# A fused attention, expert-attention and gated-MLP kernel: another written order of its pieces, and engines chosen batch by batch

## The chip, the cores and the metric

The kernel runs on one core of a Trainium2 chip. The metric is the device time of one execution in microseconds (us), as the median of several runs. The core has five instruction queues that run beside each other: TensorE (PE, with its weight loads as PEld), VectorE (DVE), ScalarE (ACT), GpSimd (POOL) and SyncE (SP), which issues DMAs. Each takes its own instructions in the order in which the program lists them, and waits on semaphores for what the others have to deliver.

## The reference, cut to what matters

Three layers follow each other, for 8 batches of 576 positions with 512 features. Everything is float32.

```python
# 1. attention, 8 heads of 64: a position sees its own block of 64 and all earlier blocks
scores = np.where(block_i >= block_j, (q @ k.T) / 8, -1e9)
x = softmax(scores) @ v
# 2. four experts, each a causal attention head of 64; the two best by gate, weighted
logits = x @ w_gate
for e in range(4):
    ye = softmax(causal((x @ wq[e]) @ (x @ wk[e]).T / 8)) @ (x @ wv[e]) @ wo[e]
    out += weight_of_e_if_in_top_2 * ye
# 3. gated MLP with a product over positions
h = np.maximum(out @ w_in, 0)
u, v = h[..., :512], h[..., 512:]
v_n = (v - mean(v)) / sqrt(var(v) + 1e-6)
v_s = einsum('ts,bsd->btd', w_spatial, v_n) + b_spatial[None, :, None]
return (u * v_s) @ w_out
```

## The kernel before, in words

Most float32 products are made of float16 halves: a number is cast to a high half, the rest is a low half, and a product is three matmuls (`PROD`). So almost each result passes through a scale or cast, usually on ScalarE, and a subtract on VectorE or GpSimd.

Work is cut into 1416 named steps, and a step into pieces of one engine each (its generator's yields). For each batch `b`, there are six pairs of heads: pairs 0 to 3 are layer 1's eight heads, pairs 4 and 5 layer 2's four experts. In the text a step is named with its batch.

- `load_qk`, `load_v` (lines 250 to 267) load a pair; `mags` (L281, or ScalarE) finds its largest magnitude; `scale1`, `scale2` make powers of two of these.
- `prep_qk` transposes q and k on TensorE (L320) and splits them (L227 on ScalarE, L233 on VectorE). `prep_v` splits v (L229, L231, L233).
- `scores` makes a pair's scores in four parts: matmuls (L369 to L388), maximum on VectorE (L391, L393), its scaling (L401 on ScalarE or L403 on VectorE), exponential on ScalarE (L407, L412).
- `weights` splits the exponentials: a cast (L327 on ScalarE, L329 on VectorE, L331 on GpSimd), and a subtract (L431, on VectorE or GpSimd). `weights_t` transposes them by DMA (L438).
- `av` multiplies by v (L448) and divides by the row sums (L464 to L471). `halves` casts (L480 on ScalarE or L482 on VectorE), subtracts (L484), and transposes by DMA (L486).
- Layer 2's own: `proj` (matmuls L803, then L813 on ScalarE and L816 on VectorE), `vproj` (L826 to L835), `gate` (L842 to L863).
- Layer 3: `hv` (matmuls L882, ScalarE L886, statistics L890 and L892), `norm0` (14 small VectorE instructions, L897 to L911), `norm` in five parts (L920 on VectorE or GpSimd, L923 on ScalarE, L926 on VectorE or GpSimd), `gating` (L961, L965), `gating2` (matmuls L977, then L980, L983, L985), `outp` (L997, L1000 and the store).
- At the start the weights are read, combined and split by steps named `su`: `su.win` and `su.wout` end in two multiplications, L530 and L531, on VectorE or GpSimd.

Nothing is decided while the kernel runs. `ORDER` is a written list of 3766 numbers; each occurrence of a number emits the next piece of that step, and an engine gets its pieces in this order. Steps of neighbouring batches are mixed in it. `WAYS` tells on which engines a step with a choice runs: one letter for one piece (`A` ScalarE, `D` VectorE, `G` GpSimd, `S` SyncE), two letters for cast and subtract. Tiles come from small pools in the order of the list; `duo`, the accumulators in PSUM, has four.

```python
    for i in ORDER:
        t = named[i]
        ...
        run(t)
```

Of the kernel before, what the change touches and what calls it, by code (L numbers as in the profile page):

```python
# [32 lines left out]
def attn_moe_gmlp_kernel(  # L33
# [17 lines left out]
    V, A, G, T = nc.vector, nc.scalar, nc.gpsimd, nc.tensor  # L51
    B, H, S, D = q.shape
# [711 lines left out]
    def dense(b, keep):  # L764
# [517 lines left out]
    def add(name, due, fn, pieces=(), deps=(), after=(), acq=(), rel=(), pdeps=None, way=None):  # L1282
# [7 lines left out]
        t = steps[name] = Step()  # L1290
# [12 lines left out]
        if way is not None:  # L1303
            ws = WAYS.get(t.place, (way,))
            t.way = ws[min(len(ws) - 1, 3 if t.b == B - 1 else min(t.b, 2))]
# [164 lines left out]
    su = startup()  # L1470
# [55 lines left out]
    for i in ORDER:  # L1526
        t = named[i]
# [45 lines left out]
```

## Time and profile before

| what | before |
|---|---|
| median of 3 runs | 1098.11 us (1095.63 to 1103.18) |
| profiled execution | 1096.49 us |
| its span, first to last instruction | 1094.8 us |
| mean granted TensorE clock | 0.933 of full speed |
| TensorE busy | 892.7 us |
| VectorE busy | 832.1 us |
| ScalarE busy | 660.9 us |
| GpSimd busy | 383.4 us |

Busy time is the union of an engine's instructions over the span. A mean over the span hides stages that differ, so stretches are read by themselves. A row of the timeline gives start and duration of some instructions of one kind, and in square brackets how long the engine had been idle before, and what ended that.

### The profile page before, as it was taken

Reading aid. Unit: us, or ns where it says so; the run is one execution under the profiler, and the core shown is the slowest. Engines: PE = TensorE matmul, PEld = TensorE weight load, DVE = VectorE, ACT = ScalarE, POOL = GpSimd, SP = SyncE. Lnnn points to the kernel's source line nnn. Section 1 sums busy time; section 2 is a strip of 40 time slices with the busy share of each in tenths; the row PEclk is TensorE's granted clock in tenths of the full one; section 3 lists DMA queues with packets and bytes.
Section 4 is the critical chain, followed back from the end, with each engine's and each line's share of the span. In section 5 each row is a group of like instructions: output and inputs, shape, how many; then the busy total and the mean of one; then the engine's idle time right before and its main releaser. Section 6 shows DMA issues by size and latency. Waiting matters only on the chain.

```text
span 1094.8 us, 25341 instructions
## 1 busy us (share of the span) xinstructions
PE 892.7 (82%) x10170; PEld 646.5 (59%) x10170; DVE 832.1 (76%) x1730; ACT 660.9 (60%) x1140; POOL 383.4 (35%) x309
## 2 busy tenths in 40 slices
PE   0466667758989799699988888997989989898978
PEld 0245555546566466466666556754767577566644
DVE  2689989999877877867777889768797887757541
ACT  2758566675667555666567668665566764536332
POOL 6054413143154221433252425543354342304210
PEclk9968787888889899899999999998999999999989
DMA  9536989699289786669929997789578537933601
GB/s 223 139 70 145 191 163 181 127 163 172 51 145 157 153 174 119 114 119 173 170 36 171 190 168 120 136 153 184 108 131 157 112 51 101 197 53 61 125 5 44
DMA packets 497719, 143.68 MB, mean 131 GB/s; under 512 B 485440, under 2 KB 491728, under 8 KB 497600
## 3 DMA queue, kind: packets, MB, share of 16 engines
q1 hardware_dynamic: 483760, 134.03, 67.3%
q0 software_dynamic: 2176, 5.25, 1.9%
q10 hardware_dynamic: 11664, 2.76, 1.6%
q8 instruction: 80, 1.31, 0.5%
q14 instruction: 39, 0.32, 0.1%
HBM read 38.19 MB, written 9.44 MB: 44 GB/s over the span
## 4 chain that ended last, share of the span: by engine, by line
PE 26%; DVE 14%; DMA 6%; ACT 6%; issue 4%; SPq 3%; POOL 2%; DVEq 0%; ACTq 0%; POOLq 0%
PE duo L977 5%; PE duo L997 5%; PE duo L448 4%; DMA pT<-p 4%; PE duo L803 2%; PE duo L882 2%; PE duo L826 2%; ACT pf L412 2%; DVE st L391 2%; PE duo L369 2%; PE duo L961 2%; SPq L438 2%; DVE vn L926 1%; DVE bs L890 1%; DVE qk L233 1%
## 5 line engine op out<-in xcount | busy, mean ns | idle before, releaser
L431 POOL TENSOR_TENSOR p<-pf,p 128x1024 f16<-128x1024 f32 (+1 forms) x106 | 205.7, 1943 | 330.5 <-ACT p L327 189.1
L412 ACT ACTIVATE pf<-duo,st,es 128x512 f32<-128x512 f32 (+3 forms) x256 | 139.8, 621 | 75.0 <-DVE st L403 58.9
L448 PEld LDWEIGHTS <-pT 128*128 128x128 f16 x4320 | 149.0, 100 | 30.4 <-DMA pT<-p 13.6
L391 DVE TENSOR_REDUCE st<-duo 128x2 f32<-128x1024 f32 (+1 forms) x192 | 150.5, 813 | 12.0 <-PE duo L377 5.9
L369 PE MATMUL duo<-qk 64*128 64x256 f16 (+3 forms) x1152 | 114.8, 313 | 45.3 <-ACT pf L412 13.6
L977 PE MATMUL duo<-wsp,vn 128*128 128x288 f16 x896 | 121.1, 289 | 10.4 <-ACT vn L923 6.3
L448 PE MATMUL duo<-v,pT 128*128 128x65 f16 (+1 forms) x2880 | 106.8, 198 | 14.6 <-DMA pT<-p 8.6
L997 PE MATMUL duo<-wo,gT 128*128 128x512 f16 (+1 forms) x480 | 111.2, 388 | 6.8 <-DVE xh L484 3.9
L977 PEld LDWEIGHTS <-vn 128*128 128x128 f16 x896 | 86.9, 98 | 35.0 <-ACT vn L923 6.9
L803 PE MATMUL duo<-x,wqk 128*128 128x288 f16 x768 | 102.5, 295 | 4.7 <-ACT pf L412 1.7
L369 PEld LDWEIGHTS <-qk 64*128 64x128 f16 x1152 | 49.4, 97 | 79.5 <-issue 56.8
L803 PEld LDWEIGHTS <-wqk 128*128 128x128 f16 x768 | 76.4, 100 | 27.1 <-issue 5.6
L997 PEld LDWEIGHTS <-gT 128*128 128x128 f16 (+1 forms) x480 | 47.5, 102 | 62.1 <-issue 12.8
L412 ACT ACTIVATE pf<-duo,st,mt 128x384 f32<-128x384 f32 (+3 forms) x128 | 69.8, 618 | 21.4 <-DVE st L403 19.9
L281 DVE TENSOR_REDUCE mst<-nat 128x1 f32<-128x640 f32 (+1 forms) x51 | 53.8, 1060 | 32.7 <-DMA nat<-in_v_dram 28.2
L327 ACT CAST p<-pf 128x1024 f16<-128x1024 f32 (+1 forms) x70 | 65.5, 943 | 12.8 <-DMA pT<-p 11.0
L331 POOL TENSOR_SCALAR p<-pf 128x1024 f16<-128x1024 f32 (+1 forms) x34 | 32.8, 965 | 112.7 <-DMA pT<-p 49.2
L826 PE MATMUL duo<-wvg,x 128*128 128x260 f16 x480 | 61.6, 290 | 8.2 <-DVE st L403 5.8
L320 PE MATMUL duo<-ident,nat 128*128 128x128 f32 (+1 forms) x320 | 53.6, 300 | 17.3 <-DVE xh L484 5.5
L233 DVE SCALAR_TENSOR_TENSOR qk<-duo,scb,qk 128x640 f16<-128x640 f32 (+1 forms) x64 | 52.6, 843 | 13.5 <-ACT qk L227 13.4
L227 ACT ACTIVATE qk<-duo,scb 128x640 f16<-128x640 f32 (+1 forms) x64 | 47.9, 768 | 24.6 <-PE duo L320 20.6
L920 POOL TENSOR_SCALAR vf<-vf,nw 128x512 f32<-128x512 f32 (+1 forms) x29 | 23.8, 831 | 110.7 <-DVE nw L911 90.0
(257 smaller groups left out, 1747.7 us busy)
## 6 DMA issues: line engine op xcount, KB each, us to landing
out_dram<-o SPq DMA_DIRECT2D x16, 512.0 KB, 3.3
nat<-in_q_dram SPq DMA_DIRECT2D x56, 128.0 KB, 3.1
nat<-in_k_dram SPq DMA_DIRECT2D x56, 128.0 KB, 3.1
nat<-in_v_dram SPq DMA_DIRECT2D x50, 128.0 KB, 2.9
wf<-in_moe_w_in_dram SPq DMA_DIRECT2D x8, 512.0 KB, 5.0
pT<-p SPq DMA_TRANSPOSE x144, 5.0
wf<-in_moe_w_out_dram SPq DMA_DIRECT2D x4, 512.0 KB, 4.9
pT<-in_moe_w_spatial_dram POOLq DMA_DIRECT2D x1, 1152.0 KB, 7.9
```

Source lines behind the costliest of these rows:

```text
L233: V.scalar_tensor_tensor(lo, src, scl, hi, op0=OP.mult, op1=OP.subtract)
L281: V.tensor_reduce(s.st[:, a, pr:pr + 1], t[:, a].rearrange("p i c d -> p i (c d)"), op=OP.max, axis=AX.X, apply_absolute_value=True)
L327: A.copy(hi, src)
L369: T.matmul(ph[:, hh, o:o + w], p.q[hs, a, ts], p.k[hs, bb, 0:w], start=i == 0, stop=False)
L391: V.reduce_max(st[:, 0, 2 * c:2 * c + 2], ph[:, :, off[c]:off[c] + P * (c + 1)], axis=AX.X)
L412: A.activation(pf[:, n * hh + off[c]:n * hh + off[c] + w], ph[:, hh, off[c]:off[c] + w], AF.Exp, bias=st[:, 1, 2 * c + hh:2 * c + hh + 1], ...
L431: (V if way[1] == "D" else G).tensor_sub(lo, src, hi)
L448: T.matmul(ps[:, hh, o:o + n], pT[:, col(t, kk):col(t, kk) + P], p.v[:, hh, kk, a:a + n], start=kk == 0 and i == 0, stop=kk == nk - 1 and ...
L803: T.matmul(ps[:, MID + a:MID + a + w], wqk16[:, l, c, 2 * n + i, :], x16[c][:, r, a:a + w], start=m == 0, stop=m == 11)
L826: T.matmul(ps[:, i, :260], x16[d][:, l, P * c:P * c + P], wvg16[:, r, d, :], start=m == 0, stop=m == 11)
L977: T.matmul(ps[:, MID + a:MID + a + n], vn[:, l, ds_], wsp16[:, r, c, a:a + n], start=i == 0, stop=False)
L997: T.matmul(ps[0:r, i], gT[:, x, d, P * c:P * c + r], wo16[:, y, d, :], start=m == 0, stop=m == 11)
```

## The change

The list of numbers is replaced by another with the same numbers, each as often as before. All pieces of a step keep their order. Of 3766 places the first 1375 move little; the sections that differ most are places 1375 to 2000, 2750 to 2875 and 3125 to 3625. `WAYS` gets up to eight entries a step, one for each batch; before, batches 0 and 1 had one each, batches 2 to 6 shared the third, and batch 7 had the fourth.

```diff
-        65, 69, 1, 68, 1, 68, 68, 68, 68, 68, 21, 23, 72, 76, 73, 66, 73, 76, 73, 76, 72, 76, 72, 72, 76, 72,
+        65, 69, 1, 68, 1, 68, 68, 68, 68, 68, 21, 23, 72, 76, 73, 66, 73, 76, 73, 76, 77, 76, 77, 77, 76, 72,
...
     WAYS = {
-        "su.win.0": ("D", "G", "G", "G"), "su.hl.0": ("D", "G", "G", "G"), "su.win.1": ("D", "G", "G", "G"),
+        "su.win.0": ("D",), "su.hl.0": ("D",), "su.win.1": ("G",), "su.hl.1": ("G",), "su.win.2": ("D",),
...
-        "w.3.1": ("DG", "AG", "AG", "DD"), "w.3.2": ("AG", "DG", "AG", "AD"), "w.3.3": ("AD", "AD", "AD", "DD"),
+        "w.3.2": ("AG", "GG", "AG", "AG", "AG", "AG", "AG", "DG"), "w.3.3": ("AD",),
...
-        "norm.2": ("GG", "DD", "GG", "DG"), "norm.3": ("GG", "DG", "GG", "DD"),
+        "norm.2": ("GG", "DG", "GG", "GG", "GG", "GG", "GG", "DD"),
+        "norm.3": ("GG", "DG", "GG", "GG", "GG", "DD", "GG", "DD"),
...
-            t.way = ws[min(len(ws) - 1, 3 if t.b == B - 1 else min(t.b, 2))]
+            t.way = ws[min(len(ws) - 1, t.b)]
```

TensorE keeps all its matmuls. By instruction, the choices of engines come to this:

| line | what | before | after |
|---|---|---|---|
| L431 | subtract of `weights`, GpSimd / VectorE | 106 / 86 | 96 / 96 |
| L327, L329, L331 | cast of `weights`, ScalarE / VectorE / GpSimd | 112 / 46 / 34 | 116 / 40 / 36 |
| L401, L403 | scaled maximum, ScalarE / VectorE | 56 / 136 | 66 / 126 |
| L480, L482 | cast of `halves`, ScalarE / VectorE | 38 / 10 | 44 / 4 |
| L530, L531 | weights' conversion, GpSimd / VectorE | 8 / 16 | 12 / 12 |
| L920 | `norm`, GpSimd / VectorE | 29 / 11 | 27 / 13 |
| L926 | `norm`, GpSimd / VectorE | 28 / 12 | 27 / 13 |
| L985 | `gating2`, GpSimd / VectorE | 20 / 12 | 19 / 13 |

All lines named here stand ahead of the list and have the same number in both files.

Three places follow, as they stand in the instruction queues before and after. The first is VectorE's queue at batch 1's `hv` and `norm0`, beside `scores` of batches 2 and 3. Before:

```order
L464 TENSOR_SCALAR rr<-duo 128x10
L466 RECIPROCAL rr<-rr 128x10
L471 TENSOR_TENSOR duo<-duo,rr 128x2x5x64
L233 SCALAR_TENSOR_TENSOR v<-nat,scb,v 128x10x64
L484 TENSOR_TENSOR xh<-duo,xh 128x2x5x64
L391 TENSOR_REDUCE st<-duo 128x2 x3
L393 TENSOR_REDUCE st<-duo 128x1
L403 TENSOR_SCALAR st<-st,mt 128x2
L403 TENSOR_SCALAR st<-st,mt 128x1
L890 BN_STATS bs_5414<-vf 128x6
L890 BN_STATS bs_5415<-vf 128x6
```

After, from the maximum that comes ahead of the same statistics:

```order
L391 TENSOR_REDUCE st<-duo 128x2
L890 BN_STATS bs_5275<-vf 128x6
L890 BN_STATS bs_5276<-vf 128x6
L892 BN_AGGR mv<-bs_5275 128x2
L892 BN_AGGR mv<-bs_5276 128x2
L403 TENSOR_SCALAR st<-st,mt 128x2
L897 TENSOR_SCALAR nw<-mv 128x5
L281 TENSOR_REDUCE mst<-nat 128x2
L899 TENSOR_SCALAR nw<-nw 128x5
L281 TENSOR_REDUCE mst<-nat 128x1
L901 TENSOR_SCALAR nw<-nw 128x5
L391 TENSOR_REDUCE st<-duo 128x2 x2
```

The statistics (`vf` to `bs`) and the first instructions of `norm0` (`nw`) move ahead of `mags` (`mst`) and of the maxima; the end of `av` (`rr`, `duo`), `prep_v` (`v`) and `halves` (`xh`) of batch 3, which stood ahead, come behind.

The second is VectorE's queue at batch 6's `proj` (L816) and batch 5's `norm` (L926). Before:

```order
L816 SCALAR_TENSOR_TENSOR qk<-duo,mt,qk 128x512
L816 SCALAR_TENSOR_TENSOR qk<-duo,mt,qk 64x64 x2
L926 TENSOR_TENSOR vn<-vf,vn 64x512
L816 SCALAR_TENSOR_TENSOR qk<-duo,mt,qk 128x576
L391 TENSOR_REDUCE st<-duo 128x2
L393 TENSOR_REDUCE st<-duo 128x1
```

After:

```order
L920 TENSOR_SCALAR vf<-vf,nw 128x512
L816 SCALAR_TENSOR_TENSOR qk<-duo,mt,qk 128x512
L816 SCALAR_TENSOR_TENSOR qk<-duo,mt,qk 64x64 x2
L926 TENSOR_TENSOR vn<-vf,vn 128x512
L816 SCALAR_TENSOR_TENSOR qk<-duo,mt,qk 128x576
L926 TENSOR_TENSOR vn<-vf,vn 64x512
L391 TENSOR_REDUCE st<-duo 128x2
```

The L816 of 576 columns moves ahead of the L926 of 64 partitions, and the fourth `norm` (L920 and an L926 of 128 partitions) has come from GpSimd.

The third is ScalarE's queue at batch 7's `scores` of pair 3 (`es`) and batch 6's of pair 5 (`mt`), with `outp` of batch 5 (L1000). Before:

```order
L412 ACTIVATE pf<-duo,st,es 128x384 x2
L412 ACTIVATE pf<-duo,st,es 128x128 x2
L1000 ACTIVATE o<-duo,hs 128x1024
L401 ACTIVATE st<-st,ln_178,es 128x1
L407 ACTIVATE duo<-duo,st,es 128x576
L401 ACTIVATE st<-st,ln_178,es 128x2
L412 ACTIVATE pf<-duo,st,es 128x256 x2
L412 ACTIVATE pf<-duo,st,mt 128x512 x2
```

After:

```order
L412 ACTIVATE pf<-duo,st,es 128x384 x2
L412 ACTIVATE pf<-duo,st,es 128x128 x2
L401 ACTIVATE st<-st,ln_178,es 128x1
L412 ACTIVATE pf<-duo,st,es 128x256 x2
L407 ACTIVATE duo<-duo,st,es 128x576
L480 CAST xh<-duo 128x2x5x64
L327 CAST p_140<-duo 128x640
L1000 ACTIVATE o<-duo,hs 128x1024
```

The exponentials of the last two parts of pair 3 (256 and 576 columns) move ahead of `outp`.

## Rows read from the trace of the kernel before

**Rows 1.** The page, part 1: busy time and share of the span by engine.

```profile
PE 892.7 (82%) x10170; PEld 646.5 (59%) x10170; DVE 832.1 (76%) x1730; ACT 660.9 (60%) x1140; POOL 383.4 (35%) x309
```

**Rows 2.** Windows: stretch, length, then busy us (instructions): PE, PEld, DVE, ACT, POOL; granted clock; DMA.

```profile
48.00:256.00 208.00, 142.63 (x1643) 112.37 (x1643) 191.60 (x350) 136.12 (x239) 74.38 (x53) 0.79 0.79 149
390.00:564.00 174.00, 151.36 (x1825) 109.95 (x1822) 133.56 (x297) 104.75 (x178) 54.73 (x37) 0.97 0.73 132
564.00:753.00 189.00, 165.33 (x2036) 117.73 (x2036) 148.90 (x312) 129.34 (x217) 88.01 (x66) 0.98 0.86 156
753.00:785.00 32.00, 29.99 (x336) 20.89 (x333) 24.74 (x76) 22.32 (x44) 7.81 (x7) 0.94 0.65 127
855.00:1012.00 157.00, 143.71 (x1596) 104.93 (x1591) 115.56 (x247) 90.20 (x165) 47.81 (x38) 0.98 0.58 99
```

**Rows 3.** Groups by line and form: busy us, mean ns, then idle before and releasers.

```profile
L431 POOL TENSOR_TENSOR p<-pf,p 128x1024 f16<-128x1024 f32 x79 | 173.3, 2195 | 255.8 <-ACT p L327 162.3 <-DVE p L329 55.3 <-issue 14.8
...
L431 DVE TENSOR_TENSOR p<-pf,p 128x1024 f16<-128x1024 f32 x17 | 21.9, 1288 | 7.8 <-ACT p L327 5.0 <-POOL p L331 2.0 <-issue 0.8
...
L926 DVE TENSOR_TENSOR vn<-vf,vn 64x512 f16<-64x512 f32 x6 | 14.9, 2486 | 3.3 <-ACT vn L923 3.2
...
L482 DVE CAST xh<-duo 128x640 f16<-128x640 f32 x10 | 8.2, 818 | 0.2
...
L926 DVE TENSOR_TENSOR vn<-vf,vn 128x512 f16<-128x512 f32 x6 | 5.2, 882 | 1.3 <-ACT vn L923 1.3
...
L531 DVE TENSOR_TENSOR x<-x,sg 128x512 f32<-128x512 f32 x6 | 4.2, 692 | 0.6
L530 DVE TENSOR_TENSOR x<-x,e 128x512 f32<-128x512 f32 x6 | 4.1, 685 | 0.1
```

**Rows 4.** Windows around 437 to 450 us, columns as in rows 2.

```profile
410.00:437.00 27.00, 25.00 (x280) 18.16 (x279) 20.97 (x57) 15.23 (x30) 3.70 (x3) 1.00 0.65 121
437.00:450.00 13.00, 3.55 (x23) 1.99 (x24) 12.69 (x32) 8.37 (x14) 4.57 (x2) 0.72 0.15 30
450.00:460.00 10.00, 10.00 (x156) 7.97 (x153) 8.02 (x15) 7.28 (x12) 4.77 (x3) 0.86 1.09 188
```

**Rows 5.** Timeline of PE, 440 to 452 us.

```profile
446.61 0.61 PE L369 MATMUL duo<-qk 64*128 64x512 f16 x2 [4.58 <-DVE qk L233]
449.59 1.04 PE L369 MATMUL duo<-qk 64*128 64x512 f16 x4 [2.36 <-DVE qk L233]
```

**Rows 6.** Timeline of DVE, 436 to 437.5 us.

```profile
436.69 1.27 DVE L890 BATCH_NORM_STATS2 bs<-vf 128x6 f32<-128x512 f32 x2
```

**Rows 7.** Timeline of PE, 890 to 964 us.

```profile
896.66 1.46 PE L369 MATMUL duo<-qk 64*128 64x512 f16 x6 [3.23 <-DVE qk L816]
...
949.98 1.52 PE L448 MATMUL duo<-v,pT 128*128 128x65 f16 x42 [2.74 <-DMA pT<-p]
...
961.43 1.44 PE L448 MATMUL duo<-V,pT 128*128 128x65 f16 x42 [1.69 <-DMA pT<-p]
```

**Rows 8.** Timeline of all engines, 886 to 896 us.

```profile
886.98 3.77 POOL L920 TENSOR_SCALAR vf<-vf,nw 128x512 f32<-128x512 f32 x5 [6.51 <-DVE nw L911]
...
890.72 4.49 POOL L926 TENSOR_TENSOR vn<-vf,vn 128x512 f16<-128x512 f32 x4
891.22 4.54 DVE L926 TENSOR_TENSOR vn<-vf,vn 64x512 f16<-64x512 f32 x1 [0.44 <-ACT vn L923]
...
895.79 0.82 DVE L816 SCALAR_TENSOR_TENSOR qk<-duo,mt,qk 128x576 f16<-128x576 f32 x1
```

**Rows 9.** Timeline of all engines, 1050 to 1060 us.

```profile
1052.15 1.87 DVE L920 TENSOR_SCALAR vf<-vf,nw 64x512 f32<-64x512 f32 x3
1052.22 1.07 POOL L920 TENSOR_SCALAR vf<-vf,nw 128x512 f32<-128x512 f32 x1 [30.23 <-DVE nw L911]
...
1054.00 1.15 PE L977 MATMUL duo<-wsp,vn 128*128 128x288 f16 x3 [5.84 <-ACT vn L923]
...
1057.75 2.34 PE L977 MATMUL duo<-wsp,vn 128*128 128x288 f16 x9 [1.53 <-POOL vn L926]
```

392 rows, old and new, of tables (ORDER, WAYS) are left out of this document.

## The prediction

> **What bounds the kernel now.** I read the page's busy times first. TensorE works 892.7 us, and VectorE 832.1 us, of a 1094.8 us span [rows 1], so no single engine fills it; an average hides two regimes, and the windows by stretch part them [rows 2]. From 48 to 256 us VectorE is busy 191.6 of 208 us (92%) and TensorE only 142.6: VectorE is the limit there. From 390 us on it turns round. TensorE is busy 151.4 of 174 us, then 165.3 of 189, 30.0 of 32, and 143.7 of 157, and VectorE 74 to 79%. From there on the end is set by TensorE's work plus the gaps in it, and an order can win only what lies in those gaps: 22.6 us between 390 and 564, 23.7 between 564 and 753, 2.0 between 753 and 785, 13.3 between 855 and 1012.
>
> The change leaves TensorE's work as it is, to the instruction. What it moves is where pieces stand. I compared the two lists place by place: positions 0 to 1375 (up to 390 us in this trace) move by 1.5 places or less on average, 1375 to 2000 (390 to 564 us) by some 10, 2000 to 2750 (564 to 753 us) by 1 to 2, 2750 to 2875 by 12, 3125 to 3500 (855 to 974 us) by 6. So the stretch 564 to 753, with 12.5% of gaps, is nearly kept, and the terms below are looked for in the others.
>
> **The change part by part.** *Start.* Two pieces of the weights' conversion (`su.win.1`, `su.wout.1`) go from VectorE to GpSimd: two instructions each, 0.685 and 0.692 us [rows 3], 2.75 us in all. Two casts of `halves` (0.818 us each) go to ScalarE: 1.64 us. Against this two weight subtracts of batch 0 come from GpSimd, 1.288 us each: 2.58 us. VectorE is left with 2.75 + 1.64 - 2.58 = 1.8 us less, in the stretch where it is the limit. I take -1.8 us. The ends are 0, if the 16 us in which VectorE does idle there take it, and -1.8. The converted weights lie on GpSimd beside 74.4 us of work in 208, so it has room [rows 2].
>
> *The jam of batch 3.* Between 437 and 450 us TensorE works 3.55 us of 13, while VectorE works 12.69 [rows 4]. The largest waits there are 4.58 and 2.36 us, for L233 of `prep_qk` of pair 3 [rows 5]: it stands in VectorE's queue behind the bn statistics of batch 1 (436.69 us [rows 6]), the 14 small instructions of `norm0`, a score maximum and two normalizations. Just before, from 410 to 437, VectorE was idle for 27.0 - 21.0 = 6.0 us [rows 4]. The new order puts `hv` of batch 1 ahead of `gating`, so that its statistics and `norm0` stand in VectorE's queue before `mags`, and can use that idle time. It pays with five other instructions of VectorE (the end of `av`, `halves` and `prep_v` of batch 3), which move from before the jam into it, about 3 us by the same forms. Nobody on TensorE waits for these soon: their products go to a later pair. The ends are 0 (as much goes in as comes out) and -9.45, TensorE's whole idle time there. I take half of the 6.0 us: -3.
>
> *The transposes of batch 7 and 6.* `av` waits 2.74 us at 949.98 and 1.69 us at 961.43 for transposed weights [rows 7]. The weights come from scores that TensorE computes, and ScalarE exponentiates, after the product `outp` of batch 5. In the new order both pairs' last scores stand ahead of an `outp`: ScalarE's exponential of the third part of pair 3 comes before L1000 of the first `outp`, not behind it. `outp` itself fills TensorE's time later just as well, and its result goes to the output, for which only the buffer waits. I take the whole, -4.4; the ends are 0 and -4.4. What could take it back is GpSimd, which now makes both halves of the first two parts.
>
> *Scores of batch 6.* At 896.66 TensorE waits 3.23 us for L816, the end of `proj` [rows 7]. That instruction stood behind L926, a subtract of 64x512 that took 4.54 us, from 891.22 to 895.76, while GpSimd ran L920 and L926 back to back from 886.98 to 895.21 [rows 8]. The mean of this form is 2.486 us against 0.882 for twice the partitions [rows 3], so VectorE is held up by GpSimd here. Now L816 comes ahead of this L926. But the fourth normalization has gone to VectorE, and its own L926 stands ahead of that same L816: the same kind of hold, by a run on GpSimd that is two instructions shorter. The ends are -3.23, and +1.3 (one more instruction of GpSimd's run, 4.49 us for four, as the later one now meets it). I take -0.5.
> On this the Trainium skill (GPSIMD Engine Reference, 1. Specifications) says that GpSimd's SBUF interfaces are shared with VectorE, with contention for VectorE instructions that have two SBUF inputs. The 4.54 us agrees. By that rule this place would gain nothing, and the sum would be 0.5 us higher; by the plain move it would gain 3.23.
>
> *The rest.* From 753 to 785 TensorE idles 2.0 us: -1, ends 0 and -2.0. Outside the jam, 390 to 564 holds 22.6 - 9.45 = 13.2 us in many short waits: -1, ends 0 and -13.2. In the tail TensorE waits 5.84 and 1.53 us for the last normalization [rows 9]. That goes to VectorE almost whole, but three of its pieces already took 1.87 us there and now there are five, and only the first product comes earlier (1.07 us on GpSimd against about 0.6): -0.4, ends 0 and -1.5. Loads that change queues are asked for tens of us ahead of use: 0.
>
> *New waits.* Re-made stretches make waits of their own. The waits that I named are 1.69 to 4.58 us long; I charge 2 us, ends 0 and 7.8 (4.58 + 3.23).
>
> **The sum**: -1.8 - 3 - 4.4 - 0.5 - 1 - 1 - 0.4 + 2 = -10.1 us. The profiled execution took 1096.49 us, 1.7 more than its span; 1096.5 - 10.1 = 1086.4. The median of the runs is 1.6 us above this execution, so the forecast is **1088**.
>
> **The rivals.** *All named waits go.* The jam gives 9.45, and 1.4 more, since the granted clock was 0.72 in it and 0.86 in the 10 us behind it [rows 4], which at the full level would be 14% of 10 us; the transposes give 4.4, batch 6 gives 3.2, the stretch from 753 gives 2.0, the start 1.8: 22.3 us, so 1074.2, or 1076 on the median's scale. For it: TensorE is the limit behind each of these places, so nothing eats the gain. Against: the jam's work on VectorE is moved, not removed.
> *The gaps come back elsewhere, no change*, 1098. For it: the stretch that is kept has 12.5% of gaps, those re-made 13.0% and 8.5% [rows 2]. They are not worse than their neighbour, so a new order may draw gaps of the same size.
> *Slower: VectorE's new subtracts are held up by GpSimd.* Twelve two-input subtracts move from GpSimd to VectorE, ten of L431 and one each of L926 and L985. If each pays what L926 pays, 2.486 - 0.882 = 1.6 us, that is 19 us; with all of it on the path and no gain 1117, with two thirds 1110. It decides where GpSimd runs without pause beside them, as in `norm` of batch 5. Against it: L431 of 1024 on VectorE took 1.288 us on average over 17 [rows 3], and a hold like that of L926 in more than a few of them would show in this mean; and ten fewer L431 run on GpSimd, at 2.195 us for the large ones [rows 3].
> The Trainium skill's same line, taken as a rule for the whole kernel, is this rival: any subtract that moves may be held, and a run on GpSimd holds all. No other row of this trace shows a hold as long as batch 5's.
>
> **How the numbers follow.** Forecast, 0.46: 1082 to 1094. All named waits go, 0.20: 1068 to 1082. No change, 0.18: 1094 to 1103. Slower, 0.16: 1103 to 1118. A measurement of this kernel tells about 1% from no change, that is 1087 and 1109. Below 1087 lie the 0.20 and 0.19 of the forecast's 0.46: faster 0.39. Above 1109 lies 0.11 of the 0.16. The rest, 0.50, is the same. The ends of all terms together give -35 to +9 us, 1063 to 1107; that all fall one way is unlikely, so the range is 1074 to 1107 and leaves out a third of the second case and most of the last.
>
> **What would show it.** Right: in the jam of batch 3 TensorE's idle time is under 7 us, and `norm0` of batch 1 begins before the scores' maxima; the two waits of L448 for transposes near the end are gone; L816 of batch 6 still waits behind a long L926. VectorE's busy time from 48 to 256 us falls by about 2 us. The tail, from the last `norm` to the end, is within 1 us. Wrong: the waits return under other names in the same stretches, then TensorE's gaps in the four stretches from 390 us on [rows 2], 61.6 us in all now, stay near 60; or VectorE's mean for L431 with two SBUF inputs rises well over 1.3 us, then it is the slower case.

## The result, and the profile after

| | before | after |
|---|---|---|
| median of 12 runs each, same chip | 1098.07 us (1090.91 to 1106.12) | 1088.11 us (1083.28 to 1091.97) |
| ratio, 95% interval | | 0.9907 [0.9886, 0.9928] |
| profiled execution, span | 1096.49, 1094.8 us | 1087.77, 1086.0 us |

The forecast was 1088. The sum agreed with the measurement; most of its terms did not, and that they came out together at the right sum was luck, as the last sections show.

The page after, part 1, and the windows of the same stretches (columns as in rows 2):

```profile
PE 894.5 (82%) x10170; PEld 649.8 (60%) x10170; DVE 832.3 (77%) x1719; ACT 666.3 (61%) x1154; POOL 374.6 (34%) x307
```

```profile
48.00:256.00 208.00, 144.01 (x1631) 113.38 (x1631) 186.70 (x336) 137.51 (x242) 72.94 (x51) 0.78 0.79 148
390.00:564.00 174.00, 154.12 (x1837) 111.56 (x1834) 141.47 (x298) 107.64 (x187) 54.88 (x37) 0.96 0.68 131
564.00:753.00 189.00, 164.80 (x2017) 118.18 (x2015) 151.91 (x309) 125.56 (x212) 81.31 (x64) 0.95 0.84 154
753.00:785.00 32.00, 31.33 (x388) 23.09 (x386) 30.02 (x82) 20.44 (x37) 13.07 (x15) 1.00 0.93 154
855.00:1012.00 157.00, 148.81 (x1685) 110.38 (x1685) 114.52 (x254) 95.53 (x175) 48.11 (x37) 0.99 0.55 99
```

TensorE's busy time is nearly what it was (892.7 us before, 894.5 now). Its gaps in the four stretches from 390 us on were 61.6 us [rows 2] and are 19.9 + 24.2 + 0.7 + 8.2 = 53.0 us: 8.6 less, and the span fell by 8.8. As the prediction said, the gain lies in gaps. The windows have fixed bounds, so the work in them is not quite the same in both traces. Which gaps changed, four views tell.

**The jam of batch 3.** TensorE's timeline and the windows about the jam, whose 13 us lie at 436 to 449 now (before: rows 4, 5):

```profile
437.08 0.90 PE L384 MATMUL duo<-qk 128*128 128x288 f16 x6 [3.66 <-ACT pf L412]
439.39 1.33 PE L320 MATMUL duo<-ident,nat 128*128 128x128 f32 x5 [1.38 <-ACT pf L412]
444.56 1.41 PE L320 MATMUL duo<-ident,nat 128*128 128x128 f32 x5 [3.85 <-DVE xh L484]
446.81 0.61 PE L369 MATMUL duo<-qk 64*128 64x512 f16 x2 [0.83 <-DVE p L431]
448.60 1.04 PE L369 MATMUL duo<-qk 64*128 64x512 f16 x4 [1.18 <-DVE qk L233]
```

```profile
436.00:449.00 13.00, 4.68 (x22) 2.76 (x23) 11.06 (x27) 8.42 (x15) 3.18 (x2) 0.59 0.21 41
```

The two waits of [rows 5] shrank from 6.94 to 2.01 us, but two L320 and an L384 ahead of them wait instead, one of them for L484, which the new order put into the jam. L484's product goes to a later pair, but L484 is also the instruction after which `halves` gives its `duo` back, and L320 writes a `duo`: TensorE waited for the buffer. All waits above 0.5 us here come to 10.9 us; before they came to 11.2 (2.15 and 2.10 beside the two shown). TensorE idles 8.3 of the 13 us; it was 9.45.

In either kernel VectorE is held here: an instruction that runs while GpSimd works takes much longer than its form does elsewhere (a hold, in what follows). VectorE and GpSimd, before and then after:

```profile
442.87 2.80 DVE L920 TENSOR_SCALAR vf<-vf,nw 128x512 f32<-128x512 f32 x2
443.09 4.57 POOL L431 TENSOR_TENSOR p<-pf,p 128x1024 f16<-128x1024 f32 x2 [10.44 <-ACT duo L407]
```

```profile
431.59 2.13 POOL L431 TENSOR_TENSOR p<-pf,p 128x1024 f16<-128x1024 f32 x1 [3.15 <-ACT p L327]
432.04 1.72 DVE L901 TENSOR_SCALAR nw<-nw 128x5 int32<-128x5 int32 x1
...
438.59 2.13 POOL L431 TENSOR_TENSOR p<-pf,p 128x1024 f16<-128x1024 f32 x1 [4.87 <-DVE p L329]
...
439.50 1.24 DVE L904 TENSOR_TENSOR nw<-nw 128x5 f32<-128x5 f32 x1
```

Before, the 14 small instructions of `norm0` took 0.16 or 0.17 us each, and two L920 took 2.80 us together (0.55 each where nothing held them). After, L901 takes 1.72 us and one L904 1.24, and the maxima stand behind L901. Every trace with the new order here has two such holds among these 14 instructions, of 0.90 to 1.72 us. So what `norm0` does earlier, it does beside a busy GpSimd; how much of the jam this makes up was not tested.

**Batch 6's scores.** Timeline of VectorE and GpSimd, against [rows 8]:

```profile
882.59 3.72 POOL L920 TENSOR_SCALAR vf<-vf,nw 128x512 f32<-128x512 f32 x4 [4.56 <-DVE nw L911]
...
884.84 0.84 DVE L926 TENSOR_TENSOR vn<-vf,vn 128x512 f16<-128x512 f32 x1 [0.33 <-ACT vn L923]
886.13 0.82 DVE L816 SCALAR_TENSOR_TENSOR qk<-duo,mt,qk 128x576 f16<-128x576 f32 x1 [0.45 <-ACT qk L813]
886.29 3.38 POOL L926 TENSOR_TENSOR vn<-vf,vn 128x512 f16<-128x512 f32 x3
887.77 2.45 DVE L926 TENSOR_TENSOR vn<-vf,vn 64x512 f16<-64x512 f32 x1 [0.83 <-ACT vn L923]
```

The L926 that I expected to be held ahead of L816 took 0.84 us, beside L920 on GpSimd. L816 came through, the L926 of 64 partitions was held behind it (2.45 us), and the wait of 3.23 us [rows 7] is gone.

**The transposes.** TensorE's waits from 905 to 965 us (before: rows 7):

```profile
916.55 1.88 PE L977 MATMUL duo<-wsp,vn 128*128 128x288 f16 x14 [2.02 <-ACT u L965]
...
938.05 2.75 PE L997 MATMUL duo<-wo,gT 128*64 128x512 f16 x12 [1.25 <-ACT pf L412]
942.90 1.45 PE L448 MATMUL duo<-v,pT 128*128 128x65 f16 x42 [0.53 <-DMA pT<-p]
950.96 0.90 PE L448 MATMUL duo<-V,pT 128*128 128x65 f16 x24 [0.69 <-DMA pT<-p]
953.07 2.02 PE L448 MATMUL duo<-V,pT 128*128 128x65 f16 x42 [1.21 <-DMA pT<-p]
```

The waits of 2.74 and 1.69 us became 0.53, 0.69 and 1.21, and two new ones stand ahead of them: 2.02 us at L977 and 1.25 us at L997. Together 5.7 us, where there were 4.4.

**The tail.** TensorE's waits for the last normalization, against [rows 9]:

```profile
1044.89 0.66 PE L977 MATMUL duo<-wsp,vn 128*128 128x288 f16 x2 [5.31 <-ACT vn L923]
1046.14 0.42 PE L977 MATMUL duo<-wsp,vn 128*128 128x288 f16 x1 [0.59 <-DVE vn L926]
1046.77 0.66 PE L977 MATMUL duo<-wsp,vn 128*128 128x288 f16 x2 [0.21 <-ACT vn L923]
1048.66 2.34 PE L977 MATMUL duo<-wsp,vn 128*128 128x288 f16 x9 [1.23 <-DVE vn L926]
```

7.3 us, against 7.4.

### The profile page after: what moved, and what is told of

It reads as the page before. It is cut to its first block, busy times and chain, and to the rows that moved or that the text cites. A ratio compares the mean times of both kernels' runs of the same rounds, so it can differ in the third digit from the quotient of the medians.

```text
span 1086.0 us, 25340 instructions
## 1 busy us (share of the span) xinstructions
PE 894.5 (82%) x10170; PEld 649.8 (60%) x10170; DVE 832.3 (77%) x1719; ACT 666.3 (61%) x1154; POOL 374.6 (34%) x307
## 4 chain that ended last, share of the span: by engine, by line
PE 33%; DVE 14%; DMA 7%; ACT 6%; issue 4%; SPq 2%; POOL 1%; DVEq 0%; ACTq 0%; POOLq 0%
PE duo L977 7%; PE duo L997 6%; PE duo L448 5%; DMA pT<-p 5%; PE duo L803 4%; PE duo L369 3%; ACT pf L412 2%; PE duo L961 2%; DVE st L391 2%; PE duo L882 2%; PE duo L826 2%; PE duo L320 1%; DMA nat<-in_k_dram 1%; PE duo L384 1%; DMA nat<-in_v_dram 1%
## 5 line engine op out<-in xcount | busy, mean ns | idle before, releaser
L431 POOL TENSOR_TENSOR p<-pf,p 128x1024 f16<-128x1024 f32 (+1 forms) x96 | 187.3, 1954 | 326.3 <-ACT p L327 217.2
L412 ACT ACTIVATE pf<-duo,st,es 128x128 f32<-128x128 f32 (+3 forms) x256 | 139.3, 621 | 65.0 <-DVE st L403 48.1
L448 PEld LDWEIGHTS <-pT 128*128 128x128 f16 x4320 | 151.4, 101 | 29.9 <-issue 12.1
L369 PE MATMUL duo<-qk 64*128 64x256 f16 (+3 forms) x1152 | 117.6, 321 | 29.7 <-ACT pf L412 14.0
L977 PE MATMUL duo<-wsp,vn 128*128 128x288 f16 x896 | 121.7, 290 | 11.2 <-ACT vn L923 5.5
L448 PE MATMUL duo<-v,pT 128*128 128x65 f16 (+1 forms) x2880 | 108.9, 200 | 15.0 <-DMA pT<-p 7.1
L997 PE MATMUL duo<-wo,gT 128*128 128x512 f16 (+1 forms) x480 | 109.2, 383 | 8.5 <-DVE xh L484 3.9
L977 PEld LDWEIGHTS <-vn 128*128 128x128 f16 x896 | 87.1, 99 | 36.2 <-ACT vn L923 6.1
L369 PEld LDWEIGHTS <-qk 64*128 64x128 f16 x1152 | 49.9, 99 | 62.1 <-issue 44.0
L997 PEld LDWEIGHTS <-gT 128*128 128x128 f16 (+1 forms) x480 | 47.2, 101 | 62.5 <-issue 12.3
L412 ACT ACTIVATE pf<-duo,st,mt 128x384 f32<-128x384 f32 (+3 forms) x128 | 69.9, 616 | 15.0 <-DVE st L403 12.1
L331 POOL TENSOR_SCALAR p<-pf 128x1024 f16<-128x1024 f32 (+1 forms) x36 | 36.5, 1014 | 117.3 <-DMA pT<-p 62.6
L327 ACT CAST p<-pf 128x1024 f16<-128x1024 f32 (+1 forms) x71 | 66.5, 947 | 9.1 <-DMA pT<-p 7.1
L320 PE MATMUL duo<-ident,nat 128*128 128x128 f32 (+1 forms) x320 | 56.4, 314 | 17.1 <-DVE xh L484 6.4
L826 PE MATMUL duo<-wvg,x 128*128 128x260 f16 x480 | 57.6, 278 | 11.6 <-DVE st L403 5.8
L384 PE MATMUL duo<-qk 128*128 128x288 f16 x288 | 47.6, 303 | 17.5 <-ACT pf L412 13.2
```

Source lines behind the costliest of these rows:

```text
L320: T.transpose(ps[:, P * c:P * c + r], p.nat[0:r, i, c, :], ident[0:r, 0:r])
L327: A.copy(hi, src)
L369: T.matmul(ph[:, hh, o:o + w], p.q[hs, a, ts], p.k[hs, bb, 0:w], start=i == 0, stop=False)
L384: T.matmul(ps[:, MID + a:MID + a + n], p.q[:, l, 512:640], p.k[:, r, a:a + n], start=i == 0, stop=i == 2 and not (p.moe and a))
L412: A.activation(pf[:, n * hh + off[c]:n * hh + off[c] + w], ph[:, hh, off[c]:off[c] + w], AF.Exp, bias=st[:, 1, 2 * c + hh:2 * c + hh + 1], ...
L431: (V if way[1] == "D" else G).tensor_sub(lo, src, hi)
```

## The experiments

"Old" and "new" are the lists of before and after. Ratios are to the kernel before, run on the same chip; its median was 1099.61 us beside the first four kernels (`e1` to `e4`), 1099.72 beside the next four (`e5` to `e8`), 1101.87 beside the last four (`e9` to `e12`). The ratios are those on record with their 95% intervals; they are not the quotients of two medians, from which they differ by up to 0.2%.

**Order or engines?** `e1_order` has the new list with the old engines, `e2_ways` the old list with the new engines.

```diff
 e1_order:  ORDER = new   WAYS = old
 e2_ways:   ORDER = old   WAYS = new
```

> The new order with the engines of before. If the gain lies in where pieces stand (places), most of it is here: 5 to 9 us under before, ratio 0.992 to 0.995, and the waits of L448 for transposes near 950 and 961 us are short. If it lies in the engines (fewer subtracts on GpSimd that hold VectorE up), this is within 2 us of before.

> The order of before with the new engines. By the places: between 1 us under before and 4 us over it, since ways and order were not made for each other. By the engines: 6 to 10 us under before, and VectorE's mean for L403 and L926 falls.

Measured: 1097.46 us, 0.9974 [0.9948, 1.0000], and 1100.94 us, 1.0004 [0.9981, 1.0027]. Neither half gives the 0.93%. In `e1_order` the fourth normalization of batch 5 is still wholly on GpSimd, whose run then meets VectorE at batch 6's scores after all: VectorE's L897, of 128x5, took 2.09 us at 877.49. So most of the gain needs order and engines together; up to 0.5% may be the order's alone.

**Early or late?** The two lists hold the same pieces up to place 2739 and behind it, so each part can be exchanged.

```diff
 e4_late:    ORDER = old[:2739] + new[2739:]
 e5_early:   ORDER = new[:2739] + old[2739:]
 e6_batch5:  ORDER = old[:2739] + new[2739:2907] + old[2907:]
```

> Order and engines of before up to place 2739 (some 749 us), and the new ones from there to the end. By the places: 7 to 9 us under before, as the two traces part after 753 us by that much, ratio 0.992 to 0.994. If the differences are chance meetings of VectorE and GpSimd that any new order draws anew, the gain is anywhere from 0 to 8 us and the trace shows other waits than the changed kernel in the same places.

> The complement of the last of the four runs before: new order and engines up to place 2739, those of before from there on. If the parts add up, the kernel with the new late part having won 0.47%, this wins the rest of the 0.93%: 3 to 6 us under before, ratio 0.994 to 0.997. If the gain of the early part is only chance of one profile, it is within 1.5 us of before, and the parts do not add up.

> The kernel before, with the new order and engines at places 2739 to 2907 alone (the end of batch 5's vproj, hv of batch 4, scores of batch 6). By the traces so far this block runs 3.9 to 4.4 us shorter wherever it is the new one, with hv of batch 4 waiting 0.7 us in place of 2.0 and its matmuls at full clock: 2.5 to 4.5 us under before, ratio 0.996 to 0.998. The rival: what is won there is waited for again before 850 us, then within 1 us of before.

`e4_late`, `e5_early` and `e6_batch5` take the engines of a step from the same list as its places. Measured: `e4_late` 1095.45 us, 0.9953 [0.9927, 0.9979]; `e5_early` 1095.53 us, 0.9957 [0.9941, 0.9973]; `e6_batch5` 1099.92 us, 0.9999 [0.9980, 1.0019]. The parts add up: 0.47% and 0.43%. The small middle part shows nothing in the runs, though its own trace is 3.0 us shorter at that place.

**The one instruction at batch 6's scores**, in the kernel before:

```diff
 L816 SCALAR_TENSOR_TENSOR qk<-duo,mt,qk 64x64 x2
-L926 TENSOR_TENSOR vn<-vf,vn 64x512
 L816 SCALAR_TENSOR_TENSOR qk<-duo,mt,qk 128x576
+L926 TENSOR_TENSOR vn<-vf,vn 64x512
```

> The kernel before with two instructions of VectorE's queue exchanged: L816 of 576 columns (batch 6) ahead of L926 of 64 partitions (batch 5). By the places: the wait of 3.23 us at 896.66 goes, and the kernel takes 2 to 3 us less, ratio 0.997 to 0.998. The rival: the hold only moves on to the maximum of the next scores behind L926, TensorE waits there, and the time is that of before within 1 us.

Measured: 1098.91 us, 0.9984 [0.9960, 1.0007]. In the trace the wait of 3.23 us is gone and one of 1.91 us comes at the next L977; the runs can't tell the difference from none, nor from the 2 to 3 us expected.

**The jam.** `e7_jamback` is the changed kernel with the nine pieces of `av`, `prep_v` and `halves` of batch 3 put ahead of the last eleven instructions of `norm0` of batch 1. The statistics and the first three of `norm0` stay in front of them, so this is not the order of before. In words, the places of the list:

```diff
-    norm0 to L901 (batch 1), then av, prep_v, halves (batch 3) mixed with the rest of norm0 (batch 1)
+    norm0 to L901 (batch 1), av, prep_v, halves (batch 3), the rest of norm0 (batch 1)
```

> The changed kernel with nine pieces of batch 3 (the end of av and halves of pair 1, prep_v of pair 3; five instructions of VectorE, two of ScalarE, one DMA) put back ahead of norm0 of batch 1, before the jam of scores. If these five, some 3 us, are what eats the gain of the earlier statistics, TensorE's waits between 437 and 450 us fall by 2 to 4 us and the kernel is 1 to 3 us under the changed one, 11 to 13 under before. The rival: VectorE's chain of norm0 and the maxima sets the jam whatever stands there, the waits stay near 11 us, and the time is that of the changed kernel.

Measured: 1089.70 us, 0.9891 [0.9865, 0.9916]. TensorE's waits in the jam:

```profile
437.56 1.60 PE L384 MATMUL duo<-qk 128*128 128x288 f16 x6 [4.33 <-DVE xh L484]
440.86 0.86 PE L320 MATMUL duo<-ident,nat 128*128 128x128 f32 x5 [0.54 <-ACT pf L412]
446.67 0.61 PE L369 MATMUL duo<-qk 64*128 64x512 f16 x2 [4.95 <-ACT qk L227]
448.36 1.04 PE L369 MATMUL duo<-qk 64*128 64x512 f16 x4 [1.08 <-DVE qk L233]
```

They come to 10.9 us again, in another distribution, as the rival said; one wait is again for L484, now at an L384, which also writes a `duo`. So the five instructions that moved in are not what ate the gain, or not by where they stand among `norm0`'s. The move of `norm0` ahead of the maxima is in both kernels and was not undone in a run. In the trace of `e1_order`, which has it too, with the old engines, the waits above 0.5 us come to 8.4 us.

**The hold by GpSimd.** [rows 8] is not the only place of its kind. In the trace of before two more L926 of 64 partitions were held, 3.23 us at 670.42 and 3.97 us at 786.46. In the changed kernel the first of these places looks as follows. In the profiled execution of before, its L858 took 0.39 us and the hold fell on that L926. Timeline of VectorE, GpSimd and TensorE:

```profile
667.12 1.15 POOL L926 TENSOR_TENSOR vn<-vf,vn 128x512 f16<-128x512 f32 x1
667.15 3.23 DVE L858 TENSOR_SCALAR gs<-gs 128x5 f32<-128x5 f32 x1
668.24 2.12 POOL L431 TENSOR_TENSOR p<-pf,p 128x1024 f16<-128x1024 f32 x1
...
670.30 1.23 DVE L816 SCALAR_TENSOR_TENSOR qk<-duo,mt,qk 128x512 f16<-128x512 f32 x3
670.32 1.15 POOL L926 TENSOR_TENSOR vn<-vf,vn 128x512 f16<-128x512 f32 x1
...
671.18 1.48 PE L448 MATMUL duo<-v,pT 128*128 128x65 f16 x24 [2.89 <-DVE qk L816]
...
671.56 2.53 DVE L926 TENSOR_TENSOR vn<-vf,vn 64x512 f16<-64x512 f32 x1
```

An instruction on five columns took 3.23 us, until two of GpSimd's instructions had ended, though GpSimd went on at once with the next, and TensorE waited 2.89 us for the L816 behind it. `e8_norm4` takes VectorE's L926 of 64 partitions, the form with the long times, away from there in five batches; `e10_b3` in batch 3 alone; `e9_before4` does it in the kernel before.

```diff
 e8_norm4, in the new WAYS:
-"norm.4": ("GG", "DG", "GD", "GD", "GD", "GD", "GD", "DG"),
+"norm.4": ("GG", "DG", "GG", "GG", "GG", "GG", "GG", "DG"),
 e10_b3, in the new WAYS:
+"norm.4": ("GG", "DG", "GD", "GG", "GD", "GD", "GD", "DG"),
 e9_before4, in the old WAYS (third letter pair: batches 2 to 6):
-"norm.4": ("GG", "DG", "GD", "DD"),
+"norm.4": ("GG", "DG", "GG", "DD"),
```

> The changed kernel with the last subtract of norm (L926 of 64 partitions) of batches 2 to 6 on GpSimd in place of VectorE. If VectorE is held up there by GpSimd's own subtracts, VectorE's busy time falls by some 10 us, five instructions of 2.5 us on average, and GpSimd's rises by 7; the time falls by 1 to 4 us below the changed kernel where VectorE sets the pace. The rival: the subtract comes later on GpSimd, behind three others, gating2 waits for it, and the time is the same or up to 4 us more.

> The changed kernel, with the last normalization's subtract (L926, 64x512) on GpSimd in batch 3 alone. In the run with batches 2 to 6 the progress pulled ahead of the changed kernel's by 5.4 us between 645 and 683 us, where batch 3's stands, and by nothing lasting elsewhere. Theory 'one place': this alone gives most of it: 1084 to 1085.5 us, ratio about 0.985 to 0.987; av of pair 1 of batch 5 waits under 1 us, and L858 takes under 1.5 us. Rival 'all five places, a little each': a fifth of 3.6 us, 1087 to 1088, ratio about 0.990.

> The kernel before, with one letter a batch changed: in batches 2 to 6 the last normalization's subtract (L926, 64x512) goes from VectorE to GpSimd. Theory 'hold' (a two-input run on GpSimd stops VectorE's instruction until the run ends, and TensorE waits for what stands behind): it works without the new order too. Two of the waits behind it are on the path before: about 3.2 us at batch 6's scores and, in most profiles of the same instructions, 3.0 us at av of pair 1 of batch 5; so -4 to -6 us, ratio 0.9945 to 0.9965. Rival 'only the new order makes it pay' (before, the time won goes into the jam and the waits for transposes behind): within 0.2%, 0.998 to 1.002.

Measured: `e8_norm4` **1084.48 us, 0.9840 [0.9814, 0.9866]**, the fastest here, ahead of the changed kernel with no overlap of the intervals; `e10_b3` 1087.78 us, 0.9866 [0.9839, 0.9893], which fits the theory of one place better than that of five, though its interval meets that of `e8_norm4` and that of the changed kernel; `e9_before4` 1089.06 us, 0.9900 [0.9875, 0.9925]. One letter in the old table gives as much as the whole new order and table. The expectation for it was half of that, or less. Groups of L926 by form in `e9_before4`:

```profile
L926 POOL TENSOR_TENSOR vn<-vf,vn 128x512 f16<-128x512 f32 x26 | 30.4, 1184 | 2.7 <-ACT vn L923 2.5
...
L926 POOL TENSOR_TENSOR vn<-vf,vn 64x512 f16<-64x512 f32 x7 | 8.5, 1220 | 4.2 <-issue 3.1 <-ACT vn L923 0.7
```

and its timeline at batch 6's scores, GpSimd and VectorE:

```profile
886.07 5.85 POOL L926 TENSOR_TENSOR vn<-vf,vn 128x512 f16<-128x512 f32 x5
887.86 0.82 DVE L816 SCALAR_TENSOR_TENSOR qk<-duo,mt,qk 128x576 f16<-128x576 f32 x1 [1.73 <-ACT qk L813]
```

GpSimd pays 1.2 us a subtract on an engine that is busy 36%, and L816 runs its 0.82 us in the middle of a GpSimd run of five, unheld.

Two things about this gain stay open. VectorE's busy time is 828.1 us in `e9_before4`, 4.0 less than before, though the five subtracts that left it had taken 14.2 us there: so VectorE's other instructions took some 10 us longer than they did, and the time was won all the same. And at L858 the subtract that moved stands behind the held instruction, not ahead of it. What changes there is what follows on GpSimd: with an L926 and then an L431, L858 took 3.23 or 3.24 us in all nine traces that show this pair beside it; with two L926 in a row, 1.15 to 1.17 us in three.

**The cost doubled.** `e12_norm3` moves four more subtracts to VectorE:

```diff
-"norm.3": ("GG", "DG", "GG", "GG", "GG", "DD", "GG", "DD"),
+"norm.3": ("GG", "DG", "GD", "GD", "GD", "DD", "GD", "DD"),
```

> The changed kernel, with the suspected cost doubled: the fourth normalization's subtract (L926, 128x512) goes to VectorE in batches 2, 3, 4 and 6 as it already stands in batch 5; four subtracts more on VectorE, four fewer on GpSimd. Theory 'hold': each of them waits for GpSimd's run beside it, so their mean on VectorE rises from 0.70 to 1.5 us or more, and the time by 2 to 6 us, to 1090 to 1094 (ratio 0.992 to 0.996); the run is one instruction (1.18 us) shorter each, which takes some of it back. Rival 'a plain move': 4 x 0.70 us on VectorE, which is idle for 20% there: within 1 us of 1088, ratio 0.990 to 0.992.

Measured: 1089.76 us, 0.9890 [0.9868, 0.9911]: the rival's plain move. VectorE's L926 by form:

```profile
L926 DVE TENSOR_TENSOR vn<-vf,vn 64x512 f16<-64x512 f32 x5 | 10.3, 2062 | 1.0 <-ACT vn L923 0.8
L926 DVE TENSOR_TENSOR vn<-vf,vn 128x512 f16<-128x512 f32 x12 | 9.2, 781 | 1.8 <-ACT vn L923 1.8
```

The same subtract on twice the partitions, one normalization earlier, is hardly held (781 ns on average; of the four new ones one took 1.74 us and three 0.68), and the later one still is (2062 ns). So not each two-input subtract on VectorE pays, and my theory in the form "each pays" fell. That it depends on what GpSimd does at that moment is the likely reason; no run tests it. The run also shows that four more subtracts on VectorE cost nothing that the runs can tell, so five fewer, at 0.68 us each, are hardly what `e9_before4` gains by.

**The transposes, put back** into the changed kernel:

```diff
 e11_outp:  ORDER = new[:3315] + old[3315:3460] + new[3460:]   (these places with their old engines)
```

> The changed kernel, with the 145 places from 3315 to 3460 (batch 7's scores and weights of pair 3, batch 6's of pair 5, outp of batch 5) in the order and with the engines of before. Prediction's step 'the transposes': both waits of L448 come back (2.74 and 1.69 us) and the time rises by 4.4 us to 1092.5, ratio 0.995. The trace of after says less: it kept 0.53 + 0.69 + 1.21 us there and has a new 1.25 at outp, so +1 to +2: 1089 to 1090, ratio 0.992 to 0.9935. Rival 'as much goes elsewhere': 1088, 0.9907.

Measured: 1087.87 us, 0.9884 [0.9861, 0.9907]; no loss. Its trace, TensorE:

```profile
941.94 2.47 PE L448 MATMUL duo<-v,pT 128*128 128x65 f16 x42 [2.65 <-DMA pT<-p]
...
952.98 1.45 PE L448 MATMUL duo<-V,pT 128*128 128x65 f16 x42 [1.43 <-DMA pT<-p]
```

Both waits are back, and the 2.02 and 1.25 us of the changed kernel are gone. The new order of these places exchanged waits, and gained nothing that the runs can tell.

**Eight runs in one table.** Each cell is how much longer (+) or shorter TensorE took for the same stretch of work than in the profiled execution of before: end of the same matmuls in the two traces, subtracted, then the difference from one line to the next. Stretches are named by the times of before. One profiled execution each, so two profiles of the same instructions differ too: `e6_batch5` has those of before in all stretches but 745 to 777 and the one behind it.

| stretch, us | after | e1 | e2 | e8 | e10 | e11 | e9 | e6 |
|---|---|---|---|---|---|---|---|---|
| 0 to 480 (start, jam) | -0.5 | -1.9 | -1.3 | +0.1 | -0.4 | -1.4 | +0.1 | +2.9 |
| 480 to 630 | -4.1 | +0.6 | +0.3 | -5.3 | -3.3 | -3.6 | -1.1 | -1.0 |
| 630 to 745 | +6.2 | +1.2 | +1.3 | +2.1 | +1.1 | +5.3 | +0.8 | +4.2 |
| 745 to 777 | -4.2 | -4.3 | -1.3 | -3.4 | -2.9 | -4.3 | -1.6 | -3.0 |
| 777 to 879 | -1.1 | +2.5 | +3.9 | -1.5 | -0.8 | +0.6 | -2.9 | +0.9 |
| 879 to 904 (batch 6's scores) | -3.8 | +0.2 | -1.1 | -3.8 | -3.8 | -3.8 | -3.8 | -1.4 |
| 904 to 966 (transposes) | +0.8 | +0.7 | +0.6 | +2.6 | +2.5 | -1.3 | +0.5 | -0.2 |
| 966 to the end | -1.8 | +0.3 | +1.4 | -2.3 | -1.9 | -1.6 | -0.2 | 0.0 |
| sum | -8.5 | -0.8 | +3.9 | -11.5 | -9.5 | -10.1 | -8.2 | +2.4 |

Read along the third line: with batch 3's L926 on GpSimd (e8, e10, e9) the stretch takes 1 to 2 us more than in the one execution that was profiled before. With it on VectorE it takes 4 to 6 us more in three of the runs shown (after, e11, e6) and in the other five with it (`e3_swap`, `e4_late`, `e5_early`, `e7_jamback`, `e12_norm3`), but 1.2 and 1.3 in e1 and e2. In e2 L858 escaped, as before; in e1 it was held 3.23 us all the same and TensorE waited 2.81 us, so the line does not hang on this hold alone. Nine of the eleven traces with L926 there show the hold at L858 (after, e1, e3 to e7, e11, e12), and the trace on which the forecast rested was not one of them: there the same length fell on L926, and TensorE's wait behind it was 1.29 us.

## Why the prediction was right, and where not

The sum was -10.1 us and the medians give -10.0. That is luck: in the traces the start and the jam gave 0.5 us where 4.8 were forecast and the transposes lost 0.8 where 4.4 were to be won, while batch 6's scores, 745 to 777 and 480 to 630 gave 12.1 us together where 2.5 were forecast. What held was the frame: TensorE's work stays, and the gain lies in its gaps. Of the signs that the prediction named for being right, two came (`norm0` begins before the maxima, the tail stays within 1 us) and four did not (the jam's idle time, the two waits of L448, L816 of batch 6 waiting, VectorE's 2 us at the start). By its steps:

- **Start, -1.8.** VectorE's busy time from 48 to 256 us fell, by 4.9 us, but TensorE stood 1.4 us later at 254 us than before, and 0.4 us earlier at 366: nothing was gained that one trace can show. The end of 0 was nearer; the stretch with 92% of VectorE did not hand its saving on.
- **The jam, -3.** The step that failed most plainly. `norm0` did begin ahead of the maxima (L897 at 428.38, the maxima at 433.67), but TensorE idles 8.3 us there, not under 7: near the end "as much goes in as comes out". What was wrong is "Nobody on TensorE waits for these soon": L320 waited 3.85 us for L484, since L484 holds a `duo` until it is done. `e7_jamback` shows that putting these pieces further ahead does not help; the waits stay at 10.9 us. And the time that VectorE had idle was not free: L901 and an L904 of `norm0` took 2.96 us there beside GpSimd, against 0.33 before. How the 3 us were lost in detail stays open; `e1_order`, with 8.4 us of waits, says that the order might have won them beside other engines.
- **The transposes, -4.4.** The waits shrank (4.43 us became 2.43), but 3.27 us of new ones came, the stretch as a whole took 0.8 us more, and 2.2 to 2.9 us more in `e4_late`, `e7_jamback`, `e8_norm4`, `e10_b3` and `e12_norm3`, which have the same places. `e11_outp`, with the old places, takes 1.3 us less and costs no time. Taking the whole of two waits, and nothing for the waits that the pieces moved ahead make themselves, was the mistake.
- **Scores of batch 6, -0.5.** Mis-sized: the stretch gained 3.8 us in each version of the new order shown that has its engines too, and nothing in `e1_order`. "The same kind of hold" did not come: the L926 ahead of L816 took 0.84 us. It met L920 on GpSimd and not an L926, but that is no rule: at 544.78 and at 664.62 in the same trace an L926 and an L403 also began beside an L920 and took 4.14 and 1.89 us. Why this one was let through stays open.
- **753 to 785, -1.** The stretch gained 4.2 us, more than its idle time of 2.0. The windows of idle time hide one thing: the 24 matmuls of L882 took 6.92 us at 763.66 before and take 5.34 now, the granted clock of the window went from 0.94 to 1.00, the full level, and the wait of TensorE ahead of them from 2.01 to 0.67 us. But `e6_batch5`, which has this part alone, gained 3.0 us there in its trace and nothing in its runs (interval -2.2 to +2.1 us), so how much it is worth stays open.
- **Rest of 390 to 564, -1.** Mis-sized: between 480 and 630 us the four versions of the new order with its engines in the table gained 3.3 to 5.3 us, where e9 and e6, with the old order there, gained 1.1 and 1.0, and `e1_order`, the new order with the old engines, lost 0.6. Single waits of 1.10, 1.09, 1.88 and 1.67 us went or shrank; one of 1.41 came. The rows below show TensorE in both.
- **Tail, -0.4.** Unchanged within 0.1 us. Of what the end gained (1.8 us), 1.0 is a wait of 1.43 us at L369, for L980, which became 0.47 and which I had not named.
- **New waits, +2.** They came, and larger: 3.85 and 3.66 us in the jam, 2.02, 1.41, 1.25 us elsewhere, and others.
- **564 to 753, kept, 0.** It was kept in the list, but the trace of after took 6.2 us more between 630 and 745. `e6_batch5`, which has the instructions of before there, took 4.2 us more, so most of this is the one profile on which the forecast rested, not the change.

TensorE's waits from 530 to 600 us, before and then after:

```profile
530.84 2.12 PE L882 MATMUL duo<-wf,x 128*128 128x512 f16 x9 [1.10 <-DMA x<-xh]
534.16 2.75 PE L882 MATMUL duo<-wf,x 128*128 128x512 f16 x12 [1.09 <-ACT vf L886]
556.60 1.88 PE L977 MATMUL duo<-wsp,vn 128*128 128x288 f16 x14 [1.88 <-ACT pf L412]
...
597.59 1.62 PE L448 MATMUL duo<-V,pT 128*128 128x65 f16 x48 [1.67 <-DVE neb L213]
```

```profile
549.75 0.32 PE L369 MATMUL duo<-qk 64*128 64x384 f16 x1 [1.41 <-DVE qk L816]
```

The rival "gaps come back elsewhere" was right about the jam, the transposes and the start, and wrong about the sum. The rival "held by GpSimd" was wrong for the subtracts that moved (L431 of 1024 columns on VectorE takes 1.268 us on average over 24, against 1.288 over 17 [rows 3]), and right that holds cost time: they were already in the kernel before. `e9_before4` puts what moving five of the held subtracts is worth there at 1.0% [0.75, 1.25], some 11 us; of that the change takes out the 3.8 us at batch 6, and `e8_norm4` gets more. The prediction took batch 5's hold for the only long one; the two others of 3.97 and 3.23 us stand in the same trace. How much of the 11 us is the holds themselves, and how much what else follows from five instructions in other queues, no run parts.

The Trainium skill (SBUF — State Buffer, Who interferes with whom) says that a VectorE instruction with one SBUF input outside the two-port modes does not contend, that one with two contends with a GpSimd instruction that reads SBUF, and that the one that comes first keeps the shared ports for its whole instruction while the other blocks. The traces agree in part: the L816 of 576 columns and the L431 that reads `duo`, in PSUM, never took over 0.826 us in 64 instructions of either trace; the holds are on instructions that have all operands in SBUF. They differ in the length: 4.54 us spans four of GpSimd's instructions of 1.12 us each [rows 8], not one. And the place where that rule, as the prediction took it, gave no gain, gained 3.8 us.

## What to carry to other kernels

Before moving many pieces, look in the trace for a form whose mean is larger than that of a bigger form of the same operation; one letter on it gave here what a whole new order gave. Idle time that a queue has ahead of a jam is no gain by itself: name the wait that is next, and price it. An instruction whose product is not needed soon may still hold a buffer that is. Where unchanged stretches of two profiles differ by up to 4 us, a wait that one profile shows, or lacks, needs a second profile before it goes into a sum.

## What the runs showed of the hardware

- A small VectorE instruction can stand for several of GpSimd's instructions in a row: 128x5 in 3.23 us (0.16 us in the same trace when undisturbed), 128x2 in 1.89 us (0.22), 64x512 in 4.54 us in the trace of before (0.68). The price does not shrink with the instruction.
- Whether it is held is not set by the operation alone. L926 of 128x512 took 0.84 us beside L920 on GpSimd at 884.84; at 544.78 in the same trace L926 of 64x512 took 4.14 us, through two L926 and an L920 of GpSimd. In `e8_norm4`, `e9_before4` and `e10_b3` L858 was let in after one GpSimd instruction (1.15, 1.17 and 1.16 us), with two L926 in a row there instead of an L926 and an L431. What lets VectorE in was not settled.
- No instruction that reads `duo` was seen held: L816 took 0.82 us in the middle of 5.85 us of GpSimd's L926 in `e9_before4`.
- Two profiles of the same instructions can differ by 4.2 us in a stretch of 115 us (630 to 745, before against `e6_batch5`).
